# Spectral filter times token MLP on one Trainium2 core: the channel transform between product groups, in another order and with other tile sizes

## The chip, the cores and the metric

The kernel runs on one core of one Trainium2 chip. The metric is the device time of one execution in microseconds (us), the median of several runs. TensorE (PE in the profile) multiplies matrices, VectorE (DVE), ScalarE (ACT) and GpSimd (POOL) work element by element, SyncE (SP) issues transfers. A matmul appears in the profile as one weight load (PEld) and one matmul instruction (PE) for each pass; a full fp32 matmul has two passes, so one call in the code is two rows in the profile. A matmul of the kind fp32r has one.

## The reference, cut to what matters

```python
x = A_x                                   # (1, 2048, 512)
xn = layernorm(x)
X = rfft2(xn) * (w_r + 1j * w_i)          # over tokens and channels
s = irfft2(X, (2048, 512))
h = layernorm(xn)                         # token-mixing MLP
u = gelu(einsum("bsd,sf->bdf", h, w1) + b1)     # F = 1792
y = einsum("bdf,fs->bds", u, w2) + b2
return x + s * silu(y.transpose(0, 2, 1))
```

The output needs two things for every token and channel: the filtered signal `s`, whose last steps are an inverse transform over channels and one over the token axis, and the gate, whose last step is the product with `w2`.

## The kernel before, in words

All of the sums are in fp32 accuracy; the big products use fp32r with each operand split into a high and a low part, so that each of them is three passes (high by high, high by low, low by high).

The program has three stages. The first (to about 88 us of the profile) runs layer norm, the first token transform and part of the product with `w1`. The second (to about 205 us) finishes the product with `w1` while the filter is applied. The third, to which the change belongs, is the product with `w2`, the rest of the inverse transform, and the gate. It runs over eight **pairs** `p` of token blocks, `p` and `p + 8`. In each pair the product with `w2` is done by a Strassen-like scheme of seven products (loop over `ORDER = (1, 2, 5, 6, 3, 7, 4)`), each a **group** of 21 matmuls of 128x128 weights by 256 columns (`products`: 7 blocks of F times 3 passes). The moving operands are the tiles `fa`, `fb`, `fc` and `fd` made from `u`, and the weights are `w2f` tiles (three buffers), which ACT (high half) and DVE (low half) form for each group some groups ahead.

Between two of these groups, once in a pair, stands a **slot**, on TensorE after the group with index `k == slot` (5, that is after product 7 and ahead of product 4; in the last pair 3). In the slot stand:

- the **token transform** of the pair before, `spectral(p - 1)`: four matmuls of 64x64 weights (`y`, `cft`) by 512 columns, into banks 0 and 1 of PSUM;
- the **channel transform** of this pair, `channels(p)`, from the tile `yt` (written by ACT and DVE copies out of `ey` some groups earlier) into banks 6 and 7. It has a full form (eight matmuls of 128x128 by 128, here called F) and a folded one, which uses that an inverse transform of even frequencies repeats: **odd k** (O) are four matmuls of 128x128 by 128; **even k** (E) are sums over 64 rows of 64 columns only, in pair 0 as eight matmuls of 64x128 by 64, in pairs 2 to 6 on **quarters** of the array, as sixteen matmuls of 64x64 by 64.

After the slot, `unfolded(p)` (ACT and DVE) puts even and odd parts together into `es` and then `y`; in the folded form one ACT copy (`y<-ps`) and five DVE operations read PSUM, in the full form one ACT copy and two. `finish` multiplies the transformed tokens of the pair before by the gate and sends them out. All instructions of an engine in this part stand in the order in which the code gives them (`keep`), so the order on TensorE is the order of the calls. The weights for the group that follows the slot (`w2f`, product 4) are long formed; that group adds into the bank that `c22` (DVE, written `c<-ps,p` in the trace) reads just ahead of it, so it waits for this DVE instruction.

Who wants what next: product 5 of the next pair needs a `w2f` tile whose low half DVE makes after `finish`, `unfolded` and two sums of blocks (`a<-a,s`, `a<-a,a`), and needs the low half only for its last 7 matmuls of 21.

Of the kernel before, what the change touches and what calls it, by code (L numbers as in the profile page):

```python
# [16 lines left out]
P = 128  # L17
S, D, F = 2048, 512, 1792
# [21 lines left out]
         (3, {0: "s", 1: "gg", 2: "gg", 3: "s", 4: "ss"}))  # L40


FOLDED = (0, 2, 3, 4, 5, 6)
QUARTERS = FOLDED[1:]
BY_TOKENS = (slice(0, P),), (slice(0, 64), slice(64, P))

KD = np.concatenate([np.arange(0, 256, 4), np.arange(2, 256, 4), np.arange(1, 256, 2)])

# [95 lines left out]
def spectral_mixer_kernel(tc, x, w1, b1, w2, b2, wk, we, wx, c_f, c_ft, c_d, c_i, c_g, c_h, c_t, out):  # L144
    nc = tc.nc
    V, A, G, T, SY = nc.vector, nc.scalar, nc.gpsimd, nc.tensor, nc.sync
# [17 lines left out]
    with tc.tile_pool(name="ps", bufs=1, space=PSUM) as psp, ExitStack() as left, ExitStack() as right:  # L164
        ps = psp.tile([P, 8, 512], F32, name="ps")
# [275 lines left out]
        T = Kept(T, keep)  # L441
# [43 lines left out]
        for j in range(NJ):  # L485
# [49 lines left out]
            if more:  # L535
                low(w[1][1], raws[j + 1, 1], w[1][0])
                if FIRST <= j < FIRST + NE:
                    i = j - FIRST
# [210 lines left out]
        for n in range(8):  # L749
            a, b, c, d, e, f = PACE[n]  # L750
# [51 lines left out]
        def sums_of_blocks():  # L802
            added_up("a12", "s1")
            added_up("a11", "a12")
# [36 lines left out]
        ci = cd  # L841
# [23 lines left out]
        def banks(p):  # L865
            return ps[:, 2 + p % 2, :HD], ps[:, 4, :HD], ps[:, 5, :HD]

        def products(p, n):

            wf = ready.pop(0)  # L870
            bx, by, bz = banks(p)
            o = {1: bx, 6: bx, 7: bx, 4: bx, 2: by, 5: bz, 3: bz}[n]

            for a, (wi, ui) in enumerate(((0, 0), (0, 1), (1, 0))):
                for m, i in enumerate(FORMS):
                    T.matmul(o, wf[:, wi, i], form_parts(n, i)[ui], start=m + a == 0 and n in (1, 2, 5),
                             stop=m == NH - 1 and a == 2, skip_group_check=n in (6, 3, 7, 4))
# [25 lines left out]
        def new_sums(p):  # L903
            return (fp.tile([P, 2, 2, 2, P], F32, name=f"es{p}", tag="es"),
                    fp.tile([P, 2, 2, 2, P], F32, name=f"y{p}", tag="y"))

        def new_gates(p):
            return [fp.tile([P, D], F32, name=f"g{j}", tag="g", bufs=4) for j in (p, p + NP)]
# [6 lines left out]
        def gathered(p):  # L915


            yt = fp.tile([P, 2, 4, 2, 64], F32, name=f"yt{p}", tag="yt")
            yts[p] = yt
            for i, j in enumerate((p, p + NP)):  # L920
                for h in range(2):
                    to = yt[:, i, :, h ^ i].rearrange("p b (s c) -> p b s c", c=2)
                    yield V.tensor_copy(to, ey[:, :, h::2, j]) if i else A.activation(to, ey[:, :, h::2, j], AF.Copy)

        def even_channels(p, yt):

            for i in range(2):
                for s in range(2):  # L930
                    at = slice(128 * i + 64 * s, 128 * i + 64 * s + 64)
                    for tokens in BY_TOKENS[p in QUARTERS]:
                        for r, rows in enumerate((slice(0, 64), slice(64, P))):
                            T.matmul(ps[tokens, 6 + r, at], yt[rows, i, 2 * s].rearrange("p e c -> p (e c)")[:, tokens],
                                     ci[rows, 2 * s, :64], start=True, stop=True)
            for i in range(2):
                for s in (1, 0):
                    at = 256 + 128 * s
                    T.matmul(ps[:, 6 + i, at:at + P], yt[:, i, 2 * s + 1].rearrange("p e c -> p (e c)"), ci[:, 2 * s + 1],
                             start=True, stop=True)  # L940

        def channels(p):

            yt = yts.pop(p)
            if p in FOLDED:
                return even_channels(p, yt)
            for i in range(2):
                pe = ps[:, 6 + i].rearrange("p (h b c) -> p h b c", b=2, c=P)
                for b in range(4):
                    T.matmul(pe[:, b % 2, b // 2], yt[:, i, b].rearrange("p e c -> p (e c)"), ci[:, b],  # L950
                             start=True, stop=True)

        def unfolded(p):

            es, y = new_sums(p) if p else first_sums
            e0, e1 = (es[:, :, k].rearrange("p i b c -> p i (b c)") for k in range(2))
            if p in FOLDED:
                first, odd = ps[:, 6, :256].rearrange("p (i s c) -> p i s c", s=2, c=64), ps[:, 6:8, 256:]
                other = y.rearrange("p i h q c -> p (i h q c)")[:, :257]
                A.activation(other, ps[:, 7, :257], AF.Copy)  # L960
                other = other[:, :256].rearrange("p (i s c) -> p i s c", s=2, c=64)

                V.tensor_add(es[:, :, 1, :, :64], first, other)
                V.tensor_sub(es[:, :, 1, 0, :63:-1], first[:, :, 0], other[:, :, 0])
                V.tensor_sub(es[:, :, 1, 1, :63:-1], other[:, :, 1], first[:, :, 1])
                V.tensor_add(e0, e1, odd)
                V.tensor_sub(e1, e1, odd)
            else:
                pe = ps[:, 6:8].rearrange("p i (h k) -> p i h k", h=2)
                A.activation(e1, pe[:, :, 1], AF.Copy)  # L970
                V.tensor_add(e0, pe[:, :, 0], e1)
                V.tensor_sub(e1, pe[:, :, 0], e1)
            yield
            u, v = es[:, :, :, 0], es[:, :, :, 1]
            V.tensor_add(y[:, :, :, 0], u, v)
            yield
            V.tensor_sub(y[:, :, ::-1, 1], u, v)
            ys[p] = y.rearrange("p i h q c -> p i (h q c)")
            yield

        def spectral(p):

            y = ys.pop(p)
            for e, cols in enumerate((slice(0, 64), slice(64, P))):
                for r, rows in enumerate((slice(0, 64), slice(64, P))):
                    i = e ^ r
                    T.matmul(ps[cols, i], cft[rows, cols], y[rows, i], start=True, stop=True)
# [21 lines left out]
        yts, ys, pieces = {}, {}, iter(())  # L1009
        last_rows = None  # L1010

        for p in range(NP):
            j0, j1 = p, p + NP
            more = p + 1 < NP
            if p:
                gates[p] = new_gates(p)
            g0, g1 = gates[p]
            bx, by, bz = banks(p)
            slot, plan = SLOTS[min(p, 1) + (not more)]
            gathering = gathered(p)  # L1020
            for k, n in enumerate(ORDER):
                started = not p and k < 2
                if not started:
                    products(p, n)
                if n == 1 and p:
                    p1 = copied(f"p1_{p}", bx, w2p)
                elif n == 5:
                    p5 = copied(f"p5_{p}", bz, fp)
                elif n == 6:
                    v2 = copied(f"v2_{p}", bx, fp)  # L1030
                elif n == 7:
                    c22 = summed(f"c22_{p}", bx, p5)
                if not started:
                    ready.extend(w for w in [next(wforms, None)] if w is not None)
                if n == 2:
                    c11 = summed(f"c11_{p}", by, p1)
                elif n == 6:
                    gate(g0, j0, left_, c11, 1.0)
                elif n == 3:
                    gate(g0, j0, right_, summed(f"c12_{p}", bz, v2), 1.0)  # L1040
                elif n == 7:
                    gate(g1, j1, right_, c22, -1.0)
                elif n == 4:
                    gate(g1, j1, left_, bx, -1.0)
                if k == slot:
                    if p:
                        spectral(p - 1)
                    channels(p)
                    pieces = unfolded(p)
                    if p:  # L1050
                        for g, j in zip(gates.pop(p - 1), (j0 - 1, j1 - 1)):
                            finish(g, j, whole)
                for what in plan.get(k, ""):
                    next(gathering if what == "g" else pieces)
                if more and n == 7:
                    sums_of_blocks()
                if not more and k == 2:
                    xr = fp.tile([P, NH * P], F32, name="xr", tag="s1", bufs=1)[:, :D]
                    for rows, tokens in halved:
                        SY.dma_start(xr[rows], x[tokens, NJ - 1])  # L1060
                if not more and k == 5:
                    spectral(p)
                    last_rows = fp.tile([P, 2, D], F32, name="rows", tag="yt")
                    finish(g0, j0, whole)
                    finish(g1, j1, right_)
# [38 lines left out]
```

## Time and profile before

| | |
|---|---|
| median of 3 runs | 374.34 us (374.27 to 374.65) |
| the profiled execution | 374.35 us, span from first to last instruction 372.6 us |
| PE busy | 361.8 us, 97% of the span |
| DVE, ACT, POOL busy | 303.8, 210.9, 86.9 us |
| mean granted TensorE clock | 0.991 |
| chain that ended last | 96% PE |

The profile is of one execution. Where the text speaks of the PE timeline, each row gives the start in us, the time from its first start to its last end, the engine, the operation with the tile it writes and the tiles it reads, the weights' size (rows used by columns used), the moving size, and the number of instructions merged into the row. Ends of matmuls are modelled, so starts are the numbers to compare.

### The profile page before, as it was taken

The page shows a single profiled execution, that of the slowest core. Times are in us where ns is not written, and L with a number is a line of the kernel's source. Part 1 is how long each engine was busy: PE and PEld are TensorE (multiplying, and loading weights), DVE is VectorE, ACT ScalarE, POOL GpSimd, SP SyncE. Part 2 cuts the span into 40 slices and gives each one's busy share as a digit, 9 for nine tenths or more (in the row PEclk, how much of TensorE's full clock was granted, in tenths as well). Part 3 has the DMA queues.
Part 4 walks back from the last instruction along what each step waited for, and adds up shares of the span by engine and source line. Part 5 has one row for each costly group of instructions (what it writes and reads, how often), then busy time and mean ns, then how long its engine had stood idle before and what let it go on. Part 6 is the DMA issues. An engine that isn't in the chain of part 4 may idle for free.

```text
span 372.6 us, 8677 instructions
## 1 busy us (share of the span) xinstructions
PE 361.8 (97%) x3402; PEld 312.6 (84%) x3402; DVE 303.8 (82%) x582; ACT 210.9 (57%) x381; POOL 86.9 (23%) x128
## 2 busy tenths in 40 slices
PE   6999999999999999999999999999999999999991
PEld 4888888877877778777888999899999999999981
DVE  4799999964799997999985879595968787787871
ACT  3787888748634427646347685555455645464520
POOL 3133333332222102221020000040405050403031
PEclk9999999999999999999999999999999999999998
DMA  7987997406696596985494586897879898897343
GB/s 191 246 200 186 233 288 249 176 2 157 172 254 200 190 244 185 273 234 181 139 297 80 141 260 117 242 135 235 137 210 179 204 190 199 188 186 159 70 56 56
DMA packets 33289, 68.38 MB, mean 184 GB/s; under 512 B 4737, under 2 KB 19505, under 8 KB 33121
## 3 DMA queue, kind: packets, MB, share of 16 engines
q1 hardware_dynamic: 24192, 42.04, 40.7%
q0 software_dynamic: 8656, 25.27, 32.2%
q10 hardware_dynamic: 400, 0.52, 0.5%
q8 instruction: 26, 0.43, 0.5%
q14 instruction: 15, 0.11, 0.1%
HBM read 59.43 MB, written 8.13 MB: 181 GB/s over the span
## 4 chain that ended last, share of the span: by engine, by line
PE 96%; DMA 1%; DVE 1%; issue 0%; ACT 0%; DVEq 0%
PE ps L141 96%; DMA x<-in_x_dram 1%; DVE rows L141 0%; DVE stm L221 0%; ACT g L141 0%; DVE h L251 0%; ACT sdm L227 0%; DVE mvm L231 0%; DVE r0m L235 0%; DVE tm L237 0%; DVE rsm L238 0%; DVE tm L236 0%; DVE nbm L240 0%; DVE v2m L225 0%; DVE v2m L226 0%
## 5 line engine op out<-in xcount | busy, mean ns | idle before, releaser
L141 PE MATMUL ps<-h,w1h 128*128 128x512 f32 x400 | 117.4, 401 | 1.7 <-DVE nbm L240 1.7
L141 PEld LDWEIGHTS ps<-h,w1h 128*128 128x128 f32 x400 | 73.5, 190 | 21.5 <-issue 4.9
L141 PE MATMUL ps<-h,w1l 128*128 128x512 f32 x200 | 68.2, 394 | 0.0
L141 DVE TENSOR_TENSOR w2f<-a,w2f 128x896 fp32r<-128x896 f32 x36 | 39.2, 1089 | 23.3 <-ACT w2f L141 23.3
L141 PEld LDWEIGHTS ps<-h,w1l 128*128 128x128 f32 x200 | 37.8, 190 | 8.4 <-DVE w1l L449 0.4
L141 ACT ACTIVATE w2f<-a 128x896 fp32r<-128x896 f32 x36 | 36.8, 1022 | 13.1 <-ACT g L141 4.8
L141 PE MATMUL ps<-fb,w2f 128*128 128x256 f32 x336 | 42.5, 281 | 0.0
L141 PE MATMUL ps<-fa,w2f 128*128 128x256 f32 x336 | 41.9, 279 | 0.0
L141 POOL DMA_DIRECT2D s<-in_w_dram x14 | 18.2, 1300 | 98.0 <-DMA s<-in_w_dram 50.3
L141 PEld LDWEIGHTS ps<-fb,w2f 128*128 128x128 f32 x336 | 40.3, 188 | 0.8 <-issue 0.8
L141 PE MATMUL ps<-fc,w2f 128*128 128x256 f32 x336 | 40.5, 278 | 0.0
L141 PEld LDWEIGHTS ps<-fa,w2f 128*128 128x128 f32 x336 | 40.3, 188 | 0.0
L141 PEld LDWEIGHTS ps<-fc,w2f 128*128 128x128 f32 x336 | 39.8, 188 | 0.0
L141 POOL DMA_DIRECT2D out_dram<-r x28 | 23.7, 1286 | 29.5 <-DVE r L141 29.5
L157 ACT ACTIVATE w1h<-w1s 128x512 fp32r<-128x512 f32 x26 | 16.2, 632 | 21.6 <-PE ps L141 12.6
L631 POOL DMA_DIRECT2D xc<-xc x16 | 9.8, 619 | 70.0 <-ACT xc L629 55.0
L287 POOL TENSOR_TENSOR ey<-t 128x256 f32<-128x256 f32 x16 | 15.7, 981 | 43.9 <-DVE t L285 43.9
L141 ACT ACTIVATE w2f<-s 128x896 fp32r<-128x896 f32 x15 | 15.3, 1020 | 13.8 <-PE ps L141 12.4
L449 DVE TENSOR_TENSOR w1l<-w1r,w1h 128x384 fp32r<-128x384 f32 x32 | 21.2, 663 | 0.1
L141 PE MATMUL ps<-fd,w2f 128*128 128x256 f32 x168 | 20.9, 278 | 0.0
L141 DVE TENSOR_TENSOR w2f<-s,w2f 128x896 fp32r<-128x896 f32 x15 | 16.3, 1088 | 5.6 <-ACT w2f L141 5.6
L141 ACT ACTIVATE g<-c,b2t 128x256 f32<-128x256 f32 x24 | 12.1, 506 | 14.8 <-DVE c L141 14.8
(119 smaller groups left out, 602.8 us busy)
## 6 DMA issues: line engine op xcount, KB each, us to landing
a<-in_w_dram SPq DMA_DIRECT2D x22, 448.0 KB, 4.0
wt<-in_wk_dram POOLq DMA_DIRECT2D x16, 512.0 KB, 6.1
s<-in_w_dram SPq DMA_DIRECT2D x16, 448.0 KB, 4.3
s<-in_w_dram POOLq DMA_DIRECT2D x16, 448.0 KB, 6.5
w1s<-in_w_dram SPq DMA_DIRECT2D x52, 128.0 KB, 5.2
w1r<-in_w_dram SPq DMA_DIRECT2D x28, 192.0 KB, 5.8
xc<-xc POOLq DMA_DIRECT2D x16, 256.0 KB, 3.0
out_dram<-in_x_dram SPq DMA_DIRECT2D x4, 960.0 KB, 7.0
```

What stands on the lines that cost most here:

```text
L141: return lambda *args, **kw: self.keep(operation(*args, **kw))
L157: return A.activation(hi, src, AF.Copy), V.tensor_sub(lo, src, hi.bitcast(F32))
L287: G.tensor_add(ey[:, 0::3, :, j], a, b)
L449: keep(V.tensor_sub(dst, src, hi.bitcast(F32)))
L631: keep(G.dma_start(*(v.rearrange("p s t c -> p s (t c)") for v in (there[c::2], here[1 - c::2, ::-1]))))
```

## The change

It replaces the two tables of pairs by one that spells the order in the slot for each pair: O is odd k, S the token transform of the pair before, E even k on quarters, F the full form. Pair 0 had E (as eight 64x128 matmuls), O and now has O, E (sixteen on quarters); pair 1 had S, F and now O, S, E; pairs 2 to 6 had S, E, O and now O, S, E; pair 7 keeps S, F. With this pair 1 also takes the folded form of `unfolded`.

```diff
-FOLDED = (0, 2, 3, 4, 5, 6)
-QUARTERS = FOLDED[1:]
-BY_TOKENS = (slice(0, P),), (slice(0, 64), slice(64, P))
+PARTS = ("OE", *["OSE"] * 6, "SF")
...
-        def even_channels(p, yt):
+        def tokens_of(yt, i, b):
+            return yt[:, i, b].rearrange("p e c -> p (e c)")
+
+        def even_channels(p):
             for i in range(2):
                 for s in range(2):
                     at = slice(128 * i + 64 * s, 128 * i + 64 * s + 64)
-                    for tokens in BY_TOKENS[p in QUARTERS]:
+                    for e in range(2):
                         for r, rows in enumerate((slice(0, 64), slice(64, P))):
-                            T.matmul(ps[tokens, 6 + r, at], yt[rows, i, 2 * s].rearrange("p e c -> p (e c)")[:, tokens],
-                                     ci[rows, 2 * s, :64], start=True, stop=True)
+                            T.matmul(ps[64 * e:64 * e + 64, 6 + r, at], yts[p][rows, i, 2 * s, e], ci[rows, 2 * s, :64],
+                                     start=True, stop=True)
+
+        def odd_channels(p):
             for i in range(2):
                 for s in (1, 0):
                     at = 256 + 128 * s
-                    T.matmul(ps[:, 6 + i, at:at + P], yt[:, i, 2 * s + 1].rearrange("p e c -> p (e c)"), ci[:, 2 * s + 1],
-                             start=True, stop=True)
+                    T.matmul(ps[:, 6 + i, at:at + P], tokens_of(yts[p], i, 2 * s + 1), ci[:, 2 * s + 1], start=True, stop=True)
...
-            if p in FOLDED:
+            if "E" in PARTS[p]:
...
-                    if p:
-                        spectral(p - 1)
-                    channels(p)
+                    for part in PARTS[p]:
+                        {"S": spectral, "E": even_channels, "O": odd_channels, "F": channels}[part](p - (part == "S"))
+                    yts.pop(p)
                     pieces = unfolded(p)
```

On TensorE, the slot of pair 0 before, between the last matmuls of product 7 and the first of product 4 (`cd` is the transform's matrix, `yt` the gathered tile):

```order
L141 MATMUL ps<-fb_2707,w2f_0_2781 128x256
L141 MATMUL ps<-fb_2709,w2f_0_2781 128x256
L141 MATMUL ps<-cd,yt_2816 128x64 x8
L141 MATMUL ps<-cd,yt_2816 128x128 x4
L141 MATMUL ps<-fb_1480,w2f_0_2810 128x256
```

And after the change, the same place:

```order
L140 MATMUL ps<-fb_2707,w2f_0_2781 128x256
L140 MATMUL ps<-fb_2709,w2f_0_2781 128x256
L140 MATMUL ps<-cd,yt_2816 128x128 x4
L140 MATMUL ps<-cd,yt_2816 64x64 x16
L140 MATMUL ps<-fb_1480,w2f_0_2810 128x256
```

Odd k has moved ahead of even k, and even k has become twice as many matmuls of half the size; what stands right ahead of product 4 is now a quarter tile.

The slot of pair 2 on TensorE before (`y`, `cft` is the token transform of pair 1); pairs 3 to 6 read the same:

```order
L141 MATMUL ps<-fb_2709,w2f_2_3243 128x256
L141 MATMUL ps<-y_3123,cft 64x512 x4
L141 MATMUL ps<-cd,yt_3217 64x64 x16
L141 MATMUL ps<-cd,yt_3217 128x128 x4
L141 MATMUL ps<-fb_1480,w2f_2_3274 128x256
```

And after the change:

```order
L140 MATMUL ps<-fb_2709,w2f_2_3266 128x256
L140 MATMUL ps<-cd,yt_3240 128x128 x4
L140 MATMUL ps<-y_3143,cft 64x512 x4
L140 MATMUL ps<-cd,yt_3240 64x64 x16
L140 MATMUL ps<-fb_1480,w2f_2_3297 128x256
```

The same matmuls stand in another order: the full-size ones have moved from behind the quarter-size ones to ahead of them. Pair 1 reads like this after the change too, where before it had four matmuls `ps<-y,cft` and then eight of 128x128. On DVE and ACT nothing moves but in pair 1, where `unfolded` has the folded form's operations.

More of the change, by code (lines that the diff above doesn't have):

```diff
@@ L938, in even_channels @@
                     at = 256 + 128 * s
-                    T.matmul(ps[:, 6 + i, at:at + P], yt[:, i, 2 * s + 1].rearrange("p e c -> p (e c)"), ci[:, 2 * s + 1],
-                             start=True, stop=True)
+                    T.matmul(ps[:, 6 + i, at:at + P], tokens_of(yts[p], i, 2 * s + 1), ci[:, 2 * s + 1], start=True, stop=True)
         def channels(p):
-            yt = yts.pop(p)
-            if p in FOLDED:
-                return even_channels(p, yt)
             for i in range(2):
@@ L949, in channels @@
                 for b in range(4):
-                    T.matmul(pe[:, b % 2, b // 2], yt[:, i, b].rearrange("p e c -> p (e c)"), ci[:, b],
-                             start=True, stop=True)
+                    T.matmul(pe[:, b % 2, b // 2], tokens_of(yts[p], i, b), ci[:, b], start=True, stop=True)
         def unfolded(p):
@@ L956, in unfolded @@
             e0, e1 = (es[:, :, k].rearrange("p i b c -> p i (b c)") for k in range(2))
-            if p in FOLDED:
+            if "E" in PARTS[p]:
                 first, odd = ps[:, 6, :256].rearrange("p (i s c) -> p i s c", s=2, c=64), ps[:, 6:8, 256:]
```

## Prediction

> **What bounds the kernel now.** I read the page first, then the PE timeline of the third stage, and then DVE's rows around two slots.
>
> ```profile
> span 372.6 us, 8677 instructions
> PE 361.8 (97%) x3402; PEld 312.6 (84%) x3402; DVE 303.8 (82%) x582; ACT 210.9 (57%) x381; POOL 86.9 (23%) x128
> ...
> PE 96%; DMA 1%; DVE 1%; issue 0%; ACT 0%; DVEq 0%
> ```
>
> TensorE is busy nearly all the time and is 96% of the chain that ends last, so a change in its slots goes straight to the end, and time on ACT or DVE counts only where TensorE has to wait for it. The rows below are the PE timeline: groups of 21 matmuls (`w2f`), and between them the slots of pairs 0, 1, 2 and 3, the starts of those behind them (`ps<-y,cft`, S), and the token transform that ends the kernel.
>
> ```profile
> 217.46 2.63 PE L141 MATMUL ps<-fb,w2f 128*128 128x256 f32 x21
> 220.02 2.20 PE L141 MATMUL ps<-cd,yt 64*128 64x64 f32 x24
> 221.98 2.72 PE L141 MATMUL ps<-fb,w2f 128*128 128x256 f32 x21
> 224.53 2.63 PE L141 MATMUL ps<-fd,w2f 128*128 128x256 f32 x21
> ...
> 236.90 2.63 PE L141 MATMUL ps<-fb,w2f 128*128 128x256 f32 x21
> 239.46 1.09 PE L141 MATMUL ps<-y,cft 64*64 64x512 f32 x8
> 240.48 2.05 PE L141 MATMUL ps<-cd,yt 128*128 128x128 f32 x16
> 242.29 2.72 PE L141 MATMUL ps<-fb,w2f 128*128 128x256 f32 x21
> 244.85 2.63 PE L141 MATMUL ps<-fd,w2f 128*128 128x256 f32 x21
> ...
> 257.22 2.63 PE L141 MATMUL ps<-fb,w2f 128*128 128x256 f32 x21
> 259.78 1.09 PE L141 MATMUL ps<-y,cft 64*64 64x512 f32 x8
> 260.69 1.73 PE L141 MATMUL ps<-cd,yt 64*64 64x64 f32 x40
> 262.18 2.72 PE L141 MATMUL ps<-fb,w2f 128*128 128x256 f32 x21
> 264.74 2.64 PE L141 MATMUL ps<-fd,w2f 128*128 128x256 f32 x21
> 267.21 2.63 PE L141 MATMUL ps<-fa,w2f 128*128 128x256 f32 x21
> ...
> 279.66 1.09 PE L141 MATMUL ps<-y,cft 64*64 64x512 f32 x8
> ...
> 282.06 2.63 PE L141 MATMUL ps<-fb,w2f 128*128 128x256 f32 x21
> 284.53 2.54 PE L141 MATMUL ps<-fd,w2f 128*128 128x256 f32 x21
> 286.91 2.54 PE L141 MATMUL ps<-fa,w2f 128*128 128x256 f32 x21
> ...
> 298.90 1.09 PE L141 MATMUL ps<-y,cft 64*64 64x512 f32 x8
> ...
> 318.78 1.09 PE L141 MATMUL ps<-y,cft 64*64 64x512 f32 x8
> ...
> 338.02 1.09 PE L141 MATMUL ps<-y,cft 64*64 64x512 f32 x8
> ...
> 352.96 1.09 PE L141 MATMUL ps<-y,cft 64*64 64x512 f32 x8
> ...
> 360.90 1.09 PE L141 MATMUL ps<-y,cft 64*64 64x512 f32 x8
> 361.92 2.74 PE L141 MATMUL ps<-fb,w2f 128*128 128x256 f32 x21
> ```
>
> No row names idle time of PE. The reader is to see two things. First, the cost of a slot is what the distance between two groups around it has too much. Second, the groups run at **two paces**: 264.74 to 267.21 is 2.47 for 21 matmuls (0.118 each), 284.53 to 286.91 is 2.38 (0.113). The pace holds from one slot to the next: behind pair 2's slot the seven groups take 262.18 to 279.66 = 17.48, behind pair 3's 282.06 to 298.90 = 16.84, so a whole stretch at the quick pace is worth 0.64 us. From S to S it is 19.88 from pair 2 to 3, 19.24 to 4, 19.88 to 5, 19.24 to 6: slow, quick, slow, quick. The stretches behind pairs 0 (221.98 to 239.46 = 17.48) and 1 (242.29 to 259.78 = 17.49) are slow, and so is the one behind pair 6: 338.02 to 352.96 is 14.94, less the 2.40 from S to the first product as in pair 2 it is 12.54 for five groups, 17.48 x 5/7 = 12.49. That one is shorter and worth 5/7 of 0.64 = 0.46. So two of the seven stretches behind slots 0 to 6 are quick, with the same instructions in them as the others. What sets the pace is not to be seen; that it changes only in slots is.
>
> The profiled execution took 374.35 us, 0.01 over the median of the runs, so the sums below, made against it, hold for the median.
>
> **Pairs 2 to 6: the same matmuls in another order.** I split pair 2's slot with two narrower windows of the same timeline:
>
> ```profile
> 260.69 0.64 PE L141 MATMUL ps<-cd,yt 64*64 64x64 f32 x32
> ...
> 261.26 1.16 PE L141 MATMUL ps<-cd,yt 128*128 128x128 f32 x8
> ```
>
> The 32 quarter matmuls (16 calls of two passes) have all started by 261.13, and the first of the eight full ones of odd k starts at 261.26. What is paid in such a slot beside the matmuls themselves is one change from full size to quarters (257.22 to 259.78 is 2.56 for a group that takes 2.47: 0.09) and one from quarters to full size, with weights that cannot be loaded ahead. After the change odd k follows product 7 without a change of size, and the two changes stand between O and S and between E and product 4. Before: E block 260.69 to 261.26 (0.57), O block to the first product 0.92, first group behind it 2.72 modelled; sum 4.21. After: O undisturbed, 8 matmuls at 0.11 (the 16 of pair 1 take 240.48 to 242.29 = 1.81, with a reload) = 0.89; E 0.57; first group as behind the token transform that ends the kernel, 2.74 (361.92); sum 4.20. The change O to S replaces the one from product to S; a pass of odd k follows the last after 0.11 and a product's after 0.12, so I take the same 0.09. If the change costs only half as much behind 128 columns as behind 256, each slot gains 0.05; if the reload costs that much more ahead of 256 columns than ahead of 128, it loses 0.05. I take 0 for all five, with -0.25 to +0.25 as ends.
>
> **Pair 1: full form to quarters.** From group to group but one, 236.90 to 244.85 = 7.95 in pair 1, and 257.22 to 264.74 = 7.52 in pair 2, both ending in the slow pace and with the same S. The slot of pair 1 becomes one of pair 2's kind, whose order was just priced at 0: **-0.43**. It was 16 full passes, and becomes 8 full ones and 32 quarters. DVE's part grows from two operations to five. That lies beside PE's groups: in pair 2 with the folded form, what comes last behind it on DVE is the low half in the second row, for the group in the third (the first row is `c22`, for pair 0 below):
>
> ```profile
> 259.89 0.42 DVE L141 TENSOR_TENSOR c<-ps,p 128x256 f32<-128x256 f32 x1
> ...
> 268.13 1.08 DVE L141 TENSOR_TENSOR w2f<-s,w2f 128x896 fp32r<-128x896 f32 x1
> ...
> 269.68 5.11 PE L141 MATMUL ps<-fc,w2f 128*128 128x256 f32 x42
> ```
>
> and the low half at 268.13 + 1.08 = 269.21 is asked for only at the 15th matmul of the group that starts at 269.68, 14 x 0.118 = 1.65 later, at 271.33. So 2.1 are left as cover, and pair 1 will look the same. If that cover were gone, PE would wait inside that group for as long as DVE came late. End values: -0.47 to -0.35, about 0.05 more or less for the two changes of size, as above.
>
> A rule of the Trainium skill speaks against quarters here: "TensorEngine Tiling (Array Packing)", section Instruction Overhead, says that a matmul has about 60 cycles of overhead whatever its columns, and not to tile a dimension that is already small. By an estimate from that page, at 2.4 GHz 25 ns each, the 32 quarters would take 0.8 us, pair 1 would gain 0.1 and pair 0, below, 0.13, and the sum of this part would be -0.23. The row (32 starts from 260.69 to 261.13, at most 14 ns each) does not agree, and the row decides, so the rule keeps no chance of its own.
>
> **Pair 0: halves to quarters, and a wait.** There is no S in it. Before, 217.46 to 224.53 = 7.07. A slot of pair 2's kind without S: 7.52 less S (259.78 to 260.69, 0.91) = 6.61. So PE alone gains 0.46. But product 4, behind the slot, adds to the bank that `c22` reads, and in pair 0 that DVE instruction is late:
>
> ```profile
> 219.90 1.09 DVE L141 TENSOR_TENSOR w2f<-a,w2f 128x896 fp32r<-128x896 f32 x1 [1.55 <-ACT w2f L141]
> 220.91 0.41 DVE L141 TENSOR_TENSOR c<-ps,v 128x256 f32<-128x256 f32 x1
> 221.24 0.41 DVE L141 TENSOR_TENSOR c<-ps,p 128x256 f32<-128x256 f32 x1
> 221.36 0.51 ACT L141 ACTIVATE g<-c,b2t 128x256 f32<-128x256 f32 x1 [1.49 <-DVE c L141]
> ...
> 228.18 1.08 DVE L141 TENSOR_TENSOR w2f<-s,w2f 128x896 fp32r<-128x896 f32 x1
> ```
>
> `c22` is the row at 221.24 and ends at 221.65, since DVE is busy with a low half until 220.99 and with `c12` after it; neither waits for the slot. Product 4 starts at 221.98 now, 0.33 behind it. Pulled ahead by 0.46, it would stand at 221.52 with its weight load at about 221.48, so it waits for 221.65 and the time of the signal (ACT's row at 221.36 starts 0.04 behind the end of `c12`, 221.32): 221.70 or so in place of 221.48, and about 0.22 to 0.25 of the 0.46 is lost. **-0.22**; ends -0.05 (a longer signal) and -0.46 (the wait does not bite). In pair 2 `c22` (the row at 259.89 above) is not near: 260.31 against 262.18. The next cover: the low half at 228.18 + 1.08 = 229.26 is needed at the 15th matmul of
>
> ```profile
> 229.48 5.11 PE L141 MATMUL ps<-fc,w2f 128*128 128x256 f32 x42
> ```
>
> so at 231.13; 1.9 are left, and 0.46 does not use that up. The gathered tile `yt`, which odd k now reads first, stands complete in time already, since even k read all of it at 220.02.
>
> **Sum without the pace:** -0.22 - 0.43 + 0 = -0.65, so 374.35 - 0.65 = 373.70, if as many stretches are quick as before. Ends: -0.05 - 0.35 + 0.25 = -0.15 and -0.46 - 0.47 - 0.25 = -1.18. About 0.2% (0.75 us) is what a measurement of this kernel can tell from no change, so the pace decides the sign: one stretch weighs as much as all the rest.
>
> **The rivals.** What ends a slot is another thing now: before, the last thing ahead of product 4 was a full-size matmul (odd k or F) with the next weights loaded behind it; after, it is a quarter, a drain and a load. "TensorEngine Tiling (Array Packing)", section Key Properties, says that a change of tiling mode drains TensorE; the 0.09 of the row above agrees, and the count of changes is two in each slot before and after, so by that rule alone the sum stays. The trace has one place of the new kind: 360.90, S, then products at 361.92, which run in the slow pace (2.74 for the group, as against 2.72 for a first group at the slow pace).
>
> - **Forecast, as many quick stretches as before, one to three of seven.** For it: behind the slots of pairs 2 to 6 the pace came out slow, quick, slow, quick, slow, although from S to the first product it is 2.40 in pair 2 (259.78 to 262.18) and in pair 3 (279.66 to 282.06), so it hangs on a phase too fine for these rows, and another order gives another draw. One: 374.34; two: 373.70; three: 373.06. Chance 0.42.
> - **Every restart behind a quarter is slow.** Mechanism: each restart from a drain falls into the same phase, and the one such place that the trace shows is slow, as are those behind full-size slots of pairs 0 and 1. The two quick stretches are lost: 374.35 - 0.65 + 2 x 0.64 = 374.98. This is the case that ends slower than before; with pair 0's wait eating all of its gain and a worse reload in five slots it reaches 375.4. Past the 0.2% bound it is when the slots give less than 0.53. Against it: five slots with the same instructions came out both ways, so what stands in a slot does not decide alone. Chance 0.33, about half of it beyond the bound.
> - **Most restarts are quick, four to seven.** Mechanism: a restart from a drain is one and the same each time, and it is the quick phase. Four: 374.35 - 0.65 - 2 x 0.64 = 372.42; five: 371.78; all seven, with the shorter one: 374.35 - 0.65 - 4 x 0.64 - 0.46 = 370.68. Against it is the slow row at 361.92. Chance 0.22.
> - **A new wait.** DVE or `c22` holds PE in pair 1 too, and the slots give nothing while the pace is as before: 374.4 to 375. The covers of 2 us speak against it. Chance 0.03.
>
> **How the numbers follow.** The likeliest is two quick stretches: 373.7; its own range is 373.0 to 374.4. The range leaves out six or seven quick stretches and the worst of the slow case, about 0.09 each side at most: 371.7 to 375.2. Faster by over 0.2%: the third case (0.22) and a third of the first (0.13): 0.35. Slower by over 0.2%: half of the second (0.17), the fourth (0.02 of it) and 0.03 for what I have not seen, taken from the first: 0.22. The rest, 0.43, is within 0.2%.
>
> **What would show it.** In the PE timeline after: from product 7's group to the second group behind it 7.52 in pair 1, about 6.85 in pair 0 with idle time of some 0.2 ended by DVE's `c` ahead of product 4, and 7.5 as now in pairs 2 to 6, where a group is at the slow pace; O starting 0.12 behind the last product with no gap. Then the seven stretches, each at 2.47 or 2.38 for a group: their count of quick ones should give the time by 0.64 each. It is wrong if a slot of pairs 2 to 6 differs by over 0.1 at the same pace, if pair 0 gains the whole 0.46, if the pace takes a third value or changes inside a stretch, or if PE idles anywhere else.

## The result, and the profile after

The changed kernel takes 375.09 us (median of 16 runs, 374.63 to 375.74), the kernel before 374.49 us (16 runs in the same comparison, 374.18 to 374.83): a ratio of 1.0016, with a 95% interval of 1.0009 to 1.0022. That is slower by 0.6 us, clear of zero, and inside the 0.2% that the prediction drew as its bound. The profiled execution took 374.96 us. Of its page, the lines that answer to those shown of before:

```profile
span 373.1 us, 8761 instructions
PE 362.7 (97%) x3442; PEld 312.8 (84%) x3442; DVE 304.9 (82%) x585; ACT 210.9 (57%) x381; POOL 86.8 (23%) x128
...
PE 94%; DVE 1%; ACT 1%; DMA 1%; issue 1%; DVEq 0%
```

The chain now holds 94% PE: product 4 in pair 0 waits for DVE's `c`, and from there back the chain runs through DVE and ACT until 215.74, where it meets PE again. In the PE timeline, the first group of the third stage, the slots of pairs 0 and 1 with the groups around them, and then of each stretch behind a slot the group that reads `fd` (the second of seven):

```profile
205.67 2.63 PE L140 MATMUL ps<-fd,w2f 128*128 128x256 f32 x21
...
218.03 2.63 PE L140 MATMUL ps<-fb,w2f 128*128 128x256 f32 x21
220.51 1.68 PE L140 MATMUL ps<-cd,yt 128*128 128x128 f32 x40
222.29 2.65 PE L140 MATMUL ps<-fb,w2f 128*128 128x256 f32 x21
224.78 2.54 PE L140 MATMUL ps<-fd,w2f 128*128 128x256 f32 x21
...
236.68 2.54 PE L140 MATMUL ps<-fb,w2f 128*128 128x256 f32 x21
239.06 1.05 PE L140 MATMUL ps<-cd,yt 128*128 128x128 f32 x8
240.04 1.09 PE L140 MATMUL ps<-y,cft 64*64 64x512 f32 x8
240.95 0.64 PE L140 MATMUL ps<-cd,yt 64*64 64x64 f32 x32
241.52 2.74 PE L140 MATMUL ps<-fb,w2f 128*128 128x256 f32 x21
244.10 2.63 PE L140 MATMUL ps<-fd,w2f 128*128 128x256 f32 x21
...
256.47 2.63 PE L140 MATMUL ps<-fb,w2f 128*128 128x256 f32 x21
...
263.99 2.63 PE L140 MATMUL ps<-fd,w2f 128*128 128x256 f32 x21
...
283.87 2.63 PE L140 MATMUL ps<-fd,w2f 128*128 128x256 f32 x21
...
303.75 2.63 PE L140 MATMUL ps<-fd,w2f 128*128 128x256 f32 x21
...
323.63 2.64 PE L140 MATMUL ps<-fd,w2f 128*128 128x256 f32 x21
...
343.51 2.64 PE L140 MATMUL ps<-fd,w2f 128*128 128x256 f32 x21
```

The last number ahead of `PE` tells the pace: a group in the middle of a stretch is 2.54 long at the quick pace and 2.63 or 2.64 at the slow one. Behind pair 0 it is quick (224.78), behind pairs 1 to 6 slow. Before it was quick behind pairs 3 and 5. In the slots, odd k follows product 7 without a gap, as it should (236.68 to 239.06 is 2.38, a plain group), S comes 0.98 later and even k 0.91 after that.

The weight loads show the wait of pair 0, at the first group behind its slot:

```profile
222.29 1.89 PEld L140 LDWEIGHTS ps<-fb,w2f 128*128 128x128 f32 x16 [0.24 <-DVE c L140]
```

The 0.57 us by which this execution is already late when the third stage starts (205.67 against 205.09) is no part of the change: over all 19 profiles of this study that group starts between 204.63 and 206.58, in second profiles of the two kernels at 205.35 (before) and 205.20 (after). From here on "stage 3" is the time from the start of the first product to the start of the last one, which leaves this out. It was 159.29 in both profiles of before, and 159.25 in this one.

The granted clock does not make the two paces: the profile gives 1.00 for the slow stretch of before from 262.20 to 279.60 and 1.00 for the quick one from 282.10 to 298.80.

### The profile page after: what moved, and what is told of

Read it like the earlier page. It is cut to its first block, busy times and chain, and to the rows that moved or that the text cites. A ratio compares the mean times of both kernels' runs of the same rounds, so it can differ in the third digit from the quotient of the medians.

```text
span 373.1 us, 8761 instructions
## 1 busy us (share of the span) xinstructions
PE 362.7 (97%) x3442; PEld 312.8 (84%) x3442; DVE 304.9 (82%) x585; ACT 210.9 (57%) x381; POOL 86.8 (23%) x128
## 4 chain that ended last, share of the span: by engine, by line
PE 94%; DVE 1%; ACT 1%; DMA 1%; issue 1%; DVEq 0%
PE ps L140 94%; DMA x<-in_x_dram 1%; ACT w2f L140 1%; DVE stm L220 0%; ACT L140 0%; DVE rows L140 0%; DVE c L140 0%; ACT yt L140 0%; ACT g L140 0%; DVE w1l L448 0%; DVE h L250 0%; ACT sdm L226 0%; DVE mvm L230 0%; DVE r0m L234 0%; DVE rsm L237 0%
```

## The experiments

The kernels differ only in what stands in each pair's slot, so each edit is given as the table `PARTS` (H stands for even k on halves as in pair 0 before; before itself is `("HO", "SF", *["SEO"] * 5, "SF")`). For each slot the question is which pace comes **in** with the stretch ahead of it and which goes **out** with the stretch behind it.

The theories change as they fall:

- Theory 1, later A: what stands last in a slot settles the pace behind it.
- Theory 2: the pace is drawn anew in every execution.
- Theory 3: the loss lies ahead of the slots.
- Theory P: the whole inner order of a slot, with the pace that comes in, settles the pace that goes out.

The "drain" of the expectations is the wait between the last quarter matmul of a slot and the first product behind it, 0.15 us from start to start in pairs 1 and 2 of the profile after.

**The changed kernel again, and its parts.** `after_2` is unchanged.

> The changed kernel a second time, unchanged, for a second profile. Theory 1 (the pace of a stretch is settled by what ends the slot ahead of it, and is the same in every execution of a program): again one quick stretch of the seven, behind pair 0, and six slow. Theory 2 (the pace is drawn anew in every execution): another set of quick stretches, so that one profile says little of the median. Theory 3 (the 0.6 us of the medians lie ahead of the slots, where the two profiles differ by 0.57 us with the same instructions): the first product group starts at 205.7 again; if that part is only chance, it starts anywhere from 205.0 to 205.8. Ratio to before 1.0016 in all of them.

```profile
205.20 2.64 PE L140 MATMUL ps<-fd,w2f 128*128 128x256 f32 x21
...
224.41 2.63 PE L140 MATMUL ps<-fd,w2f 128*128 128x256 f32 x21
...
244.29 2.64 PE L140 MATMUL ps<-fd,w2f 128*128 128x256 f32 x21
```

Median 375.25, ratio 1.0021 (1.0012 to 1.0030). Now the stretch behind pair 0 is slow too (2.63 at 224.41), and all others again; stage 3 is 159.90, 0.61 over before; the medians differ by 0.60 in the first comparison and by 0.80 in this one. So the one quick stretch of the first profile varies from execution to execution, while the six slow ones came again. Theory 3 falls: the first group starts at 205.20 here, no later than in the second profile of before (205.35), and the loss is still there.

```diff
-PARTS = ("HO", "SF", *["SEO"] * 5, "SF")
+PARTS = ("OE", "SF", *["SEO"] * 5, "SF")    # p0_only
+PARTS = ("HO", *["SEO"] * 6, "SF")          # p1_folded
+PARTS = ("HO", "SF", *["OSE"] * 5, "SF")    # order_2to6
```

> Only pair 0 is changed: odd k, then even k on quarters; pairs 1 to 7 as before. All theories: the slot of pair 0 is 0.22 us shorter, with a wait of 0.24 for DVE's c ahead of product 4. Theory 1: the stretch behind pair 0 is quick as in the changed kernel, the ones behind pairs 3 and 5 as before, if what ends a slot decides alone: three quick, 0.86 us faster than before, ratio 0.9977. If what came in from the stretch ahead decides too, the stretches behind pairs 1 to 6 may turn out otherwise, by 0.64 us each. Theory 2: any count.

Ratio 0.9985 (0.9976 to 0.9993), 373.85 us. Pair 0's slot is shorter as expected. Its stretch is slow; those behind pairs 1, 3 and 5 are quick, stage 3 158.40. Pair 1's slot is the same as before, and now leads from a slow stretch into a quick one.

> Only pair 1 is changed: S, even k on quarters, odd k, as pairs 2 to 6 had it before; so all slots from 1 to 6 are alike, in the old order, and end on full-size matmuls. All theories: the slot of pair 1 is 0.43 us shorter at the same pace. Theory 1: two or three quick stretches, among those behind pairs 1 to 6; with two, 0.43 us faster than before, ratio 0.9989. Theory 2: any count.

```profile
224.61 2.63 PE L140 MATMUL ps<-fd,w2f 128*128 128x256 f32 x21
...
244.41 2.54 PE L140 MATMUL ps<-fd,w2f 128*128 128x256 f32 x21
...
263.74 2.64 PE L140 MATMUL ps<-fd,w2f 128*128 128x256 f32 x21
...
283.53 2.54 PE L140 MATMUL ps<-fd,w2f 128*128 128x256 f32 x21
```

Ratio 0.9975 (0.9963 to 0.9986), 373.48 us, stage 3 158.21. Slow, quick, slow, quick: three quick stretches, behind pairs 1, 3 and 5. Both of the changed kernel's new sizes, alone, are gains. In both profiles one stretch more than before is quick, which is 0.64 of the gain; the rest of the difference in stage 3 is 0.25 with pair 0 changed and 0.44 with pair 1 changed.

> Only the order in pairs 2 to 6 is changed: odd k, S, even k on quarters; pairs 0 and 1 as before. All theories: those slots take the same time as before within 0.05 each. Theory 1: each of them now ends on quarters, as in the changed kernel, where all such slots without a wait led into slow stretches: no quick stretch is left, the two of before are lost, 1.28 us slower than before, ratio 1.0034. Theory 2: any count. If the order alone were harmless and the loss came from pairs 0 and 1 or from ahead of them: ratio 1.000.

```profile
258.15 2.63 PE L140 MATMUL ps<-fb,w2f 128*128 128x256 f32 x21
...
265.66 2.64 PE L140 MATMUL ps<-fd,w2f 128*128 128x256 f32 x21
...
285.54 2.64 PE L140 MATMUL ps<-fd,w2f 128*128 128x256 f32 x21
...
345.18 2.64 PE L140 MATMUL ps<-fd,w2f 128*128 128x256 f32 x21
```

Ratio 1.0032 (1.0020 to 1.0043), 375.46 us against 374.45 (1.01 us more), and stage 3 of the profile is 160.57: 1.28 over before, two stretches of 0.64 to the hundredth, and no quick one. The slot itself costs what it did (258.15 to 265.66 is 7.51, before 7.52). The loss of the changed kernel is in the order of pairs 2 to 6, and in the profile it is all pace.

**What stands last?** All new sizes with full-size matmuls last; then the changed kernel with half of odd k (u) moved from the front (o) to the end:

```diff
+PARTS = ("EO", *["SEO"] * 6, "SF")    # all_full_last
+PARTS = ("OE", *["oSEu"] * 6, "SF")   # odd_split
```

> All of the changed kernel's sizes (quarters in pair 0, pair 1 folded), but every slot ends on full-size matmuls: even k then odd k in pair 0; S, even k, odd k in pairs 1 to 6. Theory A (a product group restarted behind a drain, that is behind a quarter tile, falls into the slow pace; behind odd k, with its weights loaded ahead, it can fall into the quick one when the stretch ahead was slow): two or three quick stretches of pairs 1 to 6, in alternation; with three, stage 3 takes 158.21 (as with pair 1 folded alone) less 0.25 for pair 0 = 157.96, and the ratio to before is 0.997. Theory B (the quick stretches have to do with the sizes, and the quarters in pair 0 or pair 1 lose them): none or one quick, ratio 0.9985 to 1.000.

Ratio 0.9977 (0.9968 to 0.9987), 373.79 us, stage 3 157.89: quick behind pairs 2, 4 and 6, so theory B falls. With pair 1 folded alone, pairs 1, 3 and 5 led into quick stretches with the same slots in pairs 1 to 6, so nothing that goes with the number of the pair (buffers that alternate, say) sets the pace either.

> The changed kernel with one thing other: in pairs 1 to 6 half of odd k (two matmuls of 128x128) moves from the front of the slot to its end, ahead of product 4. So the count of changes of size and all matmuls stay, and only what stands right ahead of the products differs. Theory A: the slow rule goes, and quick stretches appear behind some of pairs 1 to 6, up to three in alternation: up to 1.9 us faster than the changed kernel, ratio to before 0.997 to 1.000. Theory C (it is the first tile of the slot, or the length of the slot, that sets the pace): all of them stay slow, ratio 1.002.

```profile
245.66 2.63 PE L140 MATMUL ps<-fd,w2f 128*128 128x256 f32 x21
...
345.10 2.63 PE L140 MATMUL ps<-fd,w2f 128*128 128x256 f32 x21
```

Ratio 1.0013 (1.0004 to 1.0023), 375.08 us, stage 3 159.85: it ends on full-size matmuls and all seven stretches are slow. So full-size matmuls at the end are not enough for a quick stretch, against what theory A expected here.

**Another inner order.** E ahead of S, in two runs; a different slot in every pair; and S last:

```diff
+PARTS = ("EO", *["ESO"] * 6, "SF")                                      # eso, eso_2
+PARTS = ("EO", "SEO", "ESO", "SEO", "oSEu", "SEO", "SF", "SF")   # mixed
+PARTS = ("EO", *["OES"] * 6, "SF")                                      # oes
```

> Pair 0 even k then odd k; pairs 1 to 6 even k on quarters, S, then odd k: the slot ends on full-size matmuls, behind S. It asks whether a slot with the same matmuls and another inner order lets a quick stretch follow a quick one. Theory A, with the alternation a matter of what is last: slow, quick, slow, quick as with S, even k, odd k. If the inner order sets the phase too: another pattern, and a quick one behind a quick one is possible. Slots 2.60 us from the last product to the first, as in the old order.

One execution took 370.75 us, stage 3 155.99, slow behind pair 0 and quick behind all pairs from 1 on:

```profile
223.85 2.63 PE L140 MATMUL ps<-fd,w2f 128*128 128x256 f32 x21
...
243.65 2.54 PE L140 MATMUL ps<-fd,w2f 128*128 128x256 f32 x21
...
339.85 2.54 PE L140 MATMUL ps<-fd,w2f 128*128 128x256 f32 x21
```

> A slot of another kind in each pair: pair 0 even k, odd k; pair 1 S, E, O; pair 2 E, S, O; pair 3 S, E, O; pair 4 half of O, S, E, half of O; pair 5 S, E, O; pair 6 S and the full form; pair 7 as before. All end on full-size matmuls. Theory A with strict alternation: behind a quick stretch always a slow one, whatever the slot (eight of eight cases so far). If the kind of slot sets the phase: a quick one behind a quick one in pair 2, 4 or 6.

372.95 us, stage 3 157.70. Quick behind pairs 1 and 2: with E, S, O in pair 2 a quick one did follow a quick one. Then slow behind 3 (S, E, O) and 4 (half of O last), quick behind 5 (S, E, O) and 6 (S, F).

> The order even k, S, odd k in pairs 1 to 6 (even k, odd k in pair 0) a second time, timed, since its one look beat both kernels. If its pattern belongs to the program: again quick behind pairs 1 to 7 and slow behind pair 0, stage 3 of 156.0, ratio to before 0.990. If it was a draw of that execution: quick stretches in other places, and a ratio between 0.990 and 0.999.

The second profile of the same program, same rows:

```profile
224.38 2.64 PE L140 MATMUL ps<-fd,w2f 128*128 128x256 f32 x21
...
244.27 2.64 PE L140 MATMUL ps<-fd,w2f 128*128 128x256 f32 x21
...
343.70 2.64 PE L140 MATMUL ps<-fd,w2f 128*128 128x256 f32 x21
```

All slow, 375.07 us, stage 3 159.96. The six timed runs fall in two clusters, 370.18 to 371.49 (four) and 375.07 and 375.34, so the ratio, 0.9908 (0.9891 to 0.9924), tells of a mixture. Neither expectation held as written. The two profiles part at pair 1: slow comes in there in both, and E, S, O led it into quick in the first and left it slow in the second. From there on each slot kept the pace that it got. So the order E, S, O mostly keeps the pace, and one transition that differs between executions settles all that follow.

> Odd k, even k, S in pairs 1 to 6: the slot ends on quarter tiles as in the changed kernel, but on those of S, and even k stands ahead of S. Theory A (a restart behind a drain is slow): six slow stretches, stage 3 of 159.9. Theory P (the pace is a phase that the whole inner order of the slot and the pace that comes in settle; what stands last does not decide): a quick one is possible; where one appears, the restart behind S with the quick pace coming in stays quick, as at the kernel's end in three runs: up to six quick, stage 3 of 156.3.

374.72 us, stage 3 159.69, six slow stretches, and the group after the last S of the kernel quick with a quick group ahead. The six fit theories A and P alike.

> The kernel before a second time, unchanged, for a second profile. If the pattern belongs to the program: again quick behind pairs 3 and 5 alone, stage 3 of 159.3. If it is drawn in each execution, or hangs on the pace's phase at the start of stage 3: another count; three (behind pairs 1, 3 and 5, as in two runs with the same slots) would give 158.6.

374.60 us, and again quick behind pairs 3 and 5 alone, stage 3 159.29: before's pattern came in both of its profiles.

**The same last tile, another length.** The changed kernel's slot with the first four calls of even k (one **wave** over the quarters) done twice (`e`), that again behind an unchanged pair 1, three times, or two calls twice (written q here):

```diff
+PARTS = ("OE", *["OSeE"] * 6, "SF")          # wave_twice, wave_twice_2
+PARTS = ("OE", "OSE", *["OSeE"] * 5, "SF")   # wave_from_slow
+PARTS = ("OE", *["OSeeE"] * 6, "SF")         # wave_thrice
+PARTS = ("OE", *["OSqE"] * 6, "SF")          # half_wave
```

> The changed kernel with the first four matmuls of even k done twice in pairs 1 to 6 (the same result written twice), so that the slot has its order and its last tile and is 0.12 us longer. Theory A: six slow stretches, stage 3 longer by 6 x 0.12 = 0.7 than the changed kernel's. Theory P: the added time shifts the phase, and the stretches may be quick, 0.64 each; if they stay slow all the same, the length of the slot is not what matters for a slot that ends so.

```profile
224.51 2.54 PE L140 MATMUL ps<-fd,w2f 128*128 128x256 f32 x21
...
243.86 2.54 PE L140 MATMUL ps<-fd,w2f 128*128 128x256 f32 x21
...
340.63 2.54 PE L140 MATMUL ps<-fd,w2f 128*128 128x256 f32 x21
```

371.45 us in one execution, with more work: stage 3 156.03, and the stretches behind all slots are quick, pair 0's among them. The slots end on quarters and restart behind a drain as in the changed kernel, so theory A falls altogether.

> The changed kernel with the first four matmuls of even k done twice in pairs 1 to 6, a second time and timed. If that slot always leads into the quick pace: every execution near 371.4, ratio to before 0.992. If it only keeps the pace that comes in: two sorts of executions, near 371.4 and, with all stretches slow, near 375.9, by what pair 0's wait gives.

Ten of twelve runs at 375.37 to 376.20 and two at 371.47 and 371.67; the profile is of the first sort, stage 3 160.60, all slow from pair 0 on (ratio 1.0014, 0.9989 to 1.0040, again of a mixture). This slot keeps what comes in, too.

> As wave_twice, but pair 1 keeps the slot of the changed kernel, which led into a slow stretch in 11 of 11 cases in two profiles of it. So pair 2's slot with the doubled wave gets a slow stretch in. If the doubled wave always leads into the quick pace: quick behind pairs 2 to 6, slow behind 1. If it keeps what comes in: slow behind all of pairs 1 to 6.

```profile
224.12 2.54 PE L140 MATMUL ps<-fd,w2f 128*128 128x256 f32 x21
...
243.44 2.63 PE L140 MATMUL ps<-fd,w2f 128*128 128x256 f32 x21
...
263.44 2.63 PE L140 MATMUL ps<-fd,w2f 128*128 128x256 f32 x21
...
343.44 2.64 PE L140 MATMUL ps<-fd,w2f 128*128 128x256 f32 x21
```

374.82 us, stage 3 159.84. This execution gave pair 0 a quick stretch (224.12), which the expectation did not foresee, and so showed more: the changed kernel's slot in pair 1 turned quick into slow (243.44), and the slots with the doubled wave kept slow to the end.

> The changed kernel with the first four matmuls of even k done three times in pairs 1 to 6: same order, same last tile, 0.23 us longer per slot than the changed kernel. If the added length sets the phase: the stretches can be slow again, stage 3 near 161.3, or quick, near 156.8. Theory A (behind a quarter, slow): slow.

> The changed kernel with only the first two matmuls of even k (one half of the tokens) done twice in pairs 1 to 6: 0.06 us longer per slot or less. If the added length sets the phase: slow (stage 3 near 160.2) or quick (near 155.7); theory A: slow.

377.13 and 376.52 us, stage 3 161.30 and 160.52, all slow; with slow coming in, they do not tell keeping from turning slow.

**The map put to use.** One slot that turns slow into quick, then slots that keep:

```diff
+PARTS = ("HO", "SEO", *["ESO"] * 5, "SF")
```

> Pair 0 as before (even k on halves, then odd k); pair 1 S, E, O, which led from slow into quick in 14 of 17 cases; pairs 2 to 6 E, S, O, which kept the pace in all of its cases; pair 7 as before. If the map of paces holds: slow behind pair 0, quick behind pairs 1 to 7, in nearly all executions: stage 3 of 159.3 less 0.43 for pair 1, less 3 x 0.64 + 0.46 for the four stretches behind pairs 1, 2, 4 and 6, less 0.28 behind pair 7, is 156.2, about 371.3, ratio to before 0.992, with the runs in one cluster. If the patterns are chance: two clusters near 371 and 375, or in between.

```profile
224.44 2.63 PE L140 MATMUL ps<-fd,w2f 128*128 128x256 f32 x21
...
244.23 2.54 PE L140 MATMUL ps<-fd,w2f 128*128 128x256 f32 x21
...
340.43 2.54 PE L140 MATMUL ps<-fd,w2f 128*128 128x256 f32 x21
```

371.65 us (370.87 to 372.91), ratio 0.9929 (0.9912 to 0.9945), stage 3 156.21 against the 156.2 worked out ahead. Five of the six runs lie from 370.87 to 372.11 and one at 372.91; none is near 375. It beats both kernels. Counted over all 19 profiles, with pair 7's slot under S, F:

| slot | slow in: goes out slow, quick | quick in: goes out slow, quick |
|---|---|---|
| S, E, O (before, pairs 2 to 6) | 3, 15 | 13, 0 |
| O, S, E (after, pairs 1 to 6) | 16, 0 | 2, 0 |
| E, S, O | 6, 1 | 0, 11 |
| O, S, E with the wave doubled | 11, 0 | 0, 6 |
| half O, S, E, half O | 7, 0 | none |
| O, E, S | 6, 0 | none |
| S, F | 16, 2 | 0, 6 |
| O, S, E with the wave three times, or two calls twice | 12, 0 | none |
| H, O or E, O in pair 0 | 10, 0 | none |
| O, E in pair 0 (with the wait for `c22`) | 6, 3 | none |

## Why the prediction was wrong

**The work in the slots was right.** Pair 1: 236.68 to 244.10 is 7.42 with a quick group in it, 7.51 at the slow pace (7.52 in the second profile, where slow comes in); 7.95 before, -0.44 against -0.43. Pair 0: 218.03 to 224.78 is 6.75, 6.84 at the slow pace; 7.07 before, -0.23 against -0.22, with the idle 0.24 by DVE's `c` that was named. Pairs 2 to 6: 256.47 to 263.99 is 7.52 as before, against 0. The rule of the Trainium skill on an overhead for each matmul ("TensorEngine Tiling (Array Packing)", section Instruction Overhead) was rightly set aside: by it pair 1 would have gained 0.1, and it gained 0.44. The covers held: among the waits of the weight loads in stage 3, the one for `c` is the only new one.

**The pace failed, in the step "another order gives another draw".** The prediction gave the likeliest chance (0.42) to as many quick stretches as before, and took the outcomes behind pairs 2 to 6, slow, quick, slow, quick, slow, for draws. They were mostly a rule: S, E, O turned a quick pace into a slow one in 13 of 13 cases and a slow one into a quick one in 15 of 18, and the second profile of before has the same pattern. The order O, S, E never led into quick, in 18 cases. So the term that the prediction put at nothing, the change in the count of quick stretches behind pairs 2 to 6, is 2 x 0.64 = 1.28 of loss; the slots gain 0.67, and the sum is +0.61, as stage 3 of the second profile shows (159.29 to 159.90).

A part of the draw is real: two of the three times that S, E, O left slow as it was are pair 2 of before in its two profiles, which is why before has two quick stretches and pair 1 folded alone has three, and behind O, E in pair 0 the pace came out quick in 3 of 9 cases. What makes these cases differ is not known.

The measured time is that of the second rival (374.98 forecast, 375.09 measured), which had 0.33. Its number was right and its mechanism was not: it put the slow pace down to the restart behind a quarter's drain, and the doubled wave restarts just so and stayed quick, while the slots with half of odd k at the end stayed slow. The alternation was in the rows that the prediction quoted; it read "slow, quick, slow, quick" and did not ask which slot had which pace coming in.

**What stays open** is the mechanism underneath: why one order turns the pace and another keeps it. With the same slot (S, E, O; E, S, O; or S, F) and slow coming in, the starts inside the slot agree to 5 ns or better between executions that go out at different paces, and for S, E, O some agree to the nanosecond, so these rows do not show what decides. That a length added to the same slot (0.12 us) let a quick pace through, which the plain order did not in two cases of two, speaks for a phase; that is an argument, and no run shows the phase itself.

## What to carry to other kernels

Where one engine is busy throughout, ask of each gap in its work not only what it costs but what pace it leaves behind; 0.64 us (4%) on a stretch of 17 us is as much as all the matmuls that were saved here (0.67), and two such stretches were lost. When a trace shows two paces, list for each transition the pace ahead and behind before calling it chance, and take a second profile: two of these programs had executions 4 us apart, and one profile of either would have told a wrong story. A gain can be laid out with such a table, one transition that turns the pace and then ones that keep it.

## What the runs showed of the hardware

A stream of 128x128 fp32r weight loads with matmuls of 256 columns ran at one of two paces only, 0.118 us (2.47 for 21) or 0.113 us (2.38 for 21), for whole stretches of 105 to 147 matmuls, and changed only where other matmuls stood between, in all 19 profiles. The stream of the second stage, 512 columns each, ends in the profile after with these rows of the PE timeline:

```profile
204.99 0.62 PE L140 MATMUL ps<-h,w1h 128*128 128x512 f32 x2
205.44 0.39 PE L140 MATMUL ps<-h,w1l 128*128 128x512 f32 x1
```

Three of its matmuls lie between 204.99 and 205.67, 0.227 each, which is twice the quick pace. The Trainium skill, "TensorE: Matmul & The Clock Gate", section Back-to-back issue gap, gives 262 cycles for 256 columns as the gap of matmuls without their weight loads, 0.109 us by an estimate at 2.4 GHz; both measured paces of this stream with weight loads are above it, and the measurement decides. Nothing outside TensorE was seen to change it within a stretch, while ACT, DVE and transfers worked beside it.
